# A gated mix of linear attention and experts on one Trainium2 core: pads put above the tiles, first-half queries first, loads moved

## The chip, the cores and the metric

The kernel runs on one core of a Trainium2 chip. The metric is the device time of one execution in microseconds, median over the runs; a lower time is better. The core's engines are TensorE (PE, with its weight loads shown as PEld), VectorE (DVE), ScalarE (ACT), GpSimd (POOL) and SyncE (SP). SP issues most DMAs, POOL the accumulating ones and some others. Each engine works through its own queue in order and waits on semaphores.

## The reference

Cut to what matters:

```python
S, D, F, E, H = 2048, 512, 1792, 8, 32          # one batch
phi = lambda t: where(t > 0, t + 1, exp(t)) + 1e-6

q, k, v = heads(x @ wqkv)                        # 32 heads of 16
kv, z   = einsum("sd,se->de", phi(k), v), phi(k).sum(0)
a = (phi(q) @ kv / (phi(q) @ z + 1e-6)) @ wo     # linear attention

w = softmax(x @ w_gate)                          # top 8 of 8: all experts
b = sum(w[:, e] * (silu(x @ w1[e]) @ w2[e]) for e in range(E))

g = sigmoid((x * gate_w).sum(-1))
out = g * a + (1 - g) * b
```

All in float32. The kernel keeps float32 accuracy by splitting each operand of a matmul into a high and a low part (type float32r) and adding three products, high by high, high by low and low by high.

## The kernel before, in words

**Products.** Each 256 x 256-blocked product is done by a scheme with seven products of half-size blocks in place of eight (Strassen's). So an expert's first layer ("up", x @ w1) works on seven combinations of x blocks and seven of weight blocks, and so does the second ("down", h @ w2). `mm3` (L57 to L60) is one such 128 x 128 by 128 x 512 product in its three split parts; lines L58, L59 and L60 are nearly all the matmuls of the kernel.

**Stages.** `keys` (L256) works over 16 row tiles: key projection, phi, and the sums y = phi(k)^T x. `experts` (L504) is then one long loop over steps `u` (L923).

**Halves, parts and groups.** The rows are two halves of 1024. A part is one expert (or the queries, `e == E`, which are treated as one more expert) for one half, `m.parts` (L102). An expert's part has 7 groups (pairs of 128 columns of F), a query part 2. `m.groups` (L109) lists them in the order of the loop: the first half's experts (56 groups), both query parts (2 groups each), the second half's experts (56). `m.G1` is the first group of the second half's queries, 58; from there on the x blocks of the second half (`n0` to `n6`) stand in place of the first half's (`x00`, `t1`, `x01`, `t3`, `x11`, `t5`, `t6`). `x_next` (L620) loads one of them from its stash in DRAM into the tiles that its predecessor leaves free; L987 to L996 say at which steps.

**Steps.** A group takes 7 steps, one up product each (6 matmuls), in `up` (L565). The down products run behind it: at step `u` the down tick is `clock(u)`, which is `u - LAG` in the first half and `u - LAG1` in the second, with LAG = 44 and LAG1 = 72. So steps 0 to 43 hold up products alone, then up and down run together, at the switch from first to second half there are 28 steps with up products alone, and at the end 72 with down products alone: 884 steps in all. `tick` (L747) does two down products (6 matmuls) with weights `w` and moving tiles `ho`; `evict` takes the results out of PSUM, scales them with the gate weights `wb` and adds them in DRAM (`acct`, on POOL's queue).

**What else a step does.** `load(g + 2)` and `prep(g + 1, k)` (L144, L175) load and split the weights of the coming groups: `rm` and `rs` are raw tiles, `o` and `oh` the split up weights, `ws` (or a spare `ho` tile, named `wx`, while `u < LAG - 8`) the split down weights, which go to a stash in DRAM (`w2stash`). `both` says that a group loads and stashes the down weights too; that is so in the first half only, and the second half reads the same stash. The queries' down weights are `wpd`, which `state` and `fold` make at steps 5 to 10. `load_w2` (L682) brings stashed weights back, three tiles of pool `w2p` in turn; from tile 377 on, every second one goes to ring "o" of pool `w1p`. `hidden` (L547) is Silu for an expert, one ACT instruction; for a query group it is `phi` (L71), two on ACT and one on DVE, and a store to `pqd`. ACT also copies PSUM banks and makes high parts (`high`), DVE low parts (`low_h`, L674) and adds (L612, L618).

**Queries and the end.** From step 461 on `queries_first` and `queries_last` turn the stored phi(q) into the attention's scaled inputs, four blocks of 512 rows, and put them back into `pqd`. In the last 28 ticks these are the moving tiles of the query parts' down products: `load_query` brings them (POOL's queue), `load_sums` the sums of the experts from `acct`, `rows` transposes the results and writes them out. `END` is tick 784.

**Memory.** Pools `const`, `xpool`, `w1p` and `hq` are stacked from the bottom of the memory. Pools `misc` (until step 17) and `w2p` (from then on) lie at its top. `pad` (L121) takes a tile of 24 float32, 96 bytes in each partition, and fills it with zeros on POOL; it is taken first in both of these pools. The tiles of such a pool lie in the order in which they are first taken, the first lowest, and the last ends at the top. In the built program the three tiles of `w2p` start at bytes 217056, 221152 and 225248 of each partition, that is 480 past a multiple of 512; the x tiles, `o`, `ho`, `ws`, raw and `r` tiles start 128 past one; tiles of `keys`' own pool that hold row tiles 12 to 15 and phi(k) start at a multiple of 512.

## Time and profile before

| | us |
|---|---|
| median of 3 runs | 2406.38 |
| lowest, highest | 2404.95, 2407.12 |
| profiled execution, its own time | 2408.38 |
| its span, first to last instruction | 2406.5 |
| `keys`, to the first up product | 100 |
| steps with up products alone, to the first down product | 100 to 182 |
| a group of 7 steps with up and down products | 19.37 |
| a group of up products alone | 9.52 |
| last down product | 2398 |

The granted clock of PE was 0.997 over the span. How to read the profile's rows: a group row gives line, engine, operation, out<-in by tile names, shapes and count, then busy time and mean length in ns of one, then the idle time of the engine before them and what ended it. A matmul's length is from its start to its modelled end and overlaps with the next one's; so rates are read from starts. A window row gives a stretch, its length, then busy us and number of instructions of PE, PEld, DVE, ACT and POOL, the granted clock, the busy share of the 16 DMA engines and the GB/s they moved. A timeline row gives start, length and the instruction, with the idle time before it in brackets. A wait row gives who waited for whom: us in total, times, the longest. A row of DMA issues gives the issuing queue, count, size and the median us from issue to landing.

### The profile page before, as it was taken

The page shows a single profiled execution, that of the slowest core. Times are in us where ns is not written, and L with a number is a line of the kernel's source. Part 1 is how long each engine was busy: PE and PEld are TensorE (multiplying, and loading weights), DVE is VectorE, ACT ScalarE, POOL GpSimd, SP SyncE. Part 2 cuts the span into 40 slices and gives each one's busy share as a digit, 9 for nine tenths or more (in the row PEclk, how much of TensorE's full clock was granted, in tenths as well). Part 3 has the DMA queues.
Part 4 walks back from the last instruction along what each step waited for, and adds up shares of the span by engine and source line. Part 5 has one row for each costly group of instructions (what it writes and reads, how often), then busy time and mean ns, then how long its engine had stood idle before and what let it go on. Part 6 is the DMA issues. An engine that isn't in the chain of part 4 may idle for free. (4 is left out here: it accounts for less than half of the span.)

```text
span 2406.5 us, 31379 instructions
## 1 busy us (share of the span) xinstructions
PE 2378.6 (99%) x10483; PEld 1936.1 (80%) x10483; DVE 1829.2 (76%) x3107; ACT 1414.8 (59%) x2650; POOL 151.8 (6%) x218
## 2 busy tenths in 40 slices
PE   8999999999999999999999999999999999999998
PEld 8878888888888888888788888888888888888876
DVE  6788888888888888888776767677676666766678
ACT  6676666666666666666656555555555555555454
POOL 1110000000000000000110000000000000000021
PEclk9999999999999999999999999999999999999999
DMA  7898888979888888879864444554545454454577
GB/s 219 263 300 253 266 266 261 274 249 279 255 262 263 263 273 257 273 254 273 288 208 121 143 139 167 146 162 149 167 153 142 137 144 142 142 148 132 140 272 269
DMA packets 296529, 512.31 MB, mean 213 GB/s; under 512 B 24224, under 2 KB 192048, under 8 KB 295984
## 3 DMA queue, kind: packets, MB, share of 16 engines
q1 hardware_dynamic: 273536, 463.84, 58.5%
q0 software_dynamic: 22832, 46.49, 10.0%
q8 instruction: 82, 1.34, 0.2%
q14 instruction: 79, 0.65, 0.1%
HBM read 344.61 MB, written 161.42 MB: 210 GB/s over the span
## 5 line engine op out<-in xcount | busy, mean ns | idle before, releaser
L58 PE MATMUL p<-ho,w 128*128 128x512 f32 x1624 | 645.7, 398 | 2.5 <-ACT p L63 1.6
L60 PE MATMUL p<-ho,w 128*128 128x512 f32 x1624 | 645.3, 397 | 0.0
L59 PE MATMUL p<-ho,w 128*128 128x512 f32 x1624 | 638.9, 393 | 0.0
L674 DVE TENSOR_TENSOR ho<-s,ho 128x512 fp32r<-128x512 f32 x784 | 536.2, 685 | 56.4 <-ACT ho L63 54.8
L63 ACT ACTIVATE ho<-s 128x512 fp32r<-128x512 f32 x784 | 486.5, 621 | 18.8 <-PE p L60 11.7
L58 PEld LDWEIGHTS p<-ho,w 128*128 128x128 f32 x1624 | 305.1, 188 | 76.3 <-ACT p L63 6.2
L60 PEld LDWEIGHTS p<-ho,w 128*128 128x128 f32 x1624 | 304.9, 188 | 74.3
L59 PEld LDWEIGHTS p<-ho,w 128*128 128x128 f32 x1624 | 305.5, 188 | 71.5
L550 ACT ACTIVATE s<-s 128x512 f32<-128x512 f32 x224 | 141.6, 632 | 282.8 <-DVE s L612 201.7
L612 DVE TENSOR_TENSOR s<-c,s 128x512 f32<-128x512 f32 x116 | 80.2, 691 | 151.5 <-PE c L60 147.2
L63 ACT ACTIVATE o<-rm 128x512 fp32r<-128x512 f32 x240 | 136.6, 570 | 86.0 <-PE a L60 65.4
L63 ACT ACTIVATE o<-rs 128x512 fp32r<-128x512 f32 x224 | 127.4, 569 | 67.4 <-PE a L60 63.8
L63 ACT ACTIVATE ws<-rm 128x512 fp32r<-128x512 f32 (+1 forms) x217 | 122.4, 571 | 63.4 <-DMA w2stash<-ws 56.4
L618 DVE TENSOR_TENSOR s<-a,s 128x512 f32<-128x512 f32 x116 | 80.1, 691 | 81.5 <-PE a L60 81.4
L550 ACT ACTIVATE s<-b 128x512 f32<-128x512 f32 x112 | 67.2, 600 | 114.5 <-PE b L60 102.2
L63 ACT ACTIVATE s<-a 128x512 f32<-128x512 f32 x116 | 69.3, 597 | 98.8 <-PE a L60 98.8
L190 DVE TENSOR_TENSOR o<-rs,o 128x512 fp32r<-128x512 f32 x168 | 114.8, 683 | 13.8 <-ACT o L63 13.0
L190 DVE TENSOR_TENSOR o<-rm,o 128x512 fp32r<-128x512 f32 x180 | 123.1, 684 | 1.3 <-ACT o L63 1.2
L208 DVE TENSOR_TENSOR ws<-rm,ws 128x512 fp32r<-128x512 f32 x164 | 112.3, 685 | 7.7 <-ACT ws L63 7.7
L63 ACT ACTIVATE s<-c 128x512 f32<-128x512 f32 x116 | 69.1, 595 | 27.0 <-PE c L60 26.9
L63 ACT ACTIVATE b<-a 128x512 f32<-128x512 f32 x116 | 67.1, 579 | 23.9 <-PE a L60 23.8
L708 POOL DMA_DIRECT2D acct<-c x28 | 24.0, 856 | 864.2 <-DVE c L704 639.2
(291 smaller groups left out, 4525.2 us busy)
## 6 DMA issues: line engine op xcount, KB each, us to landing
w<-w2stash SPq DMA_DIRECT2D x406, 512.0 KB, 3.9
w2stash<-ws SPq DMA_DIRECT2D x381, 256.0 KB, 4.4
rm<-wm SPq DMA_DIRECT2D x224, 256.0 KB, 5.4
rs<-wm SPq DMA_DIRECT2D x112, 256.0 KB, 3.7
wb<-wgtd SPq DMA_DIRECT2D x16, 512.0 KB, 5.0
acct<-c POOLq DMA_DIRECT2D x28, 256.0 KB, 5.6
acct<-d POOLq DMA_DIRECT2D x28, 256.0 KB, 5.4
acct<-k POOLq DMA_DIRECT2D x28, 256.0 KB, 5.4
```

The lines of the kernel that those rows point to most:

```text
L58: nc.tensor.matmul(ps, wh, xh, start=start, stop=False, skip_group_check=True)
L59: nc.tensor.matmul(ps, wh, xl, start=False, stop=False, skip_group_check=True)
L60: nc.tensor.matmul(ps, wlo, xh, start=False, stop=stop, skip_group_check=True)
L63: nc.scalar.activation(dst, src, AF.Copy, scale=scale, bias=bias)
L190: v.tensor_sub(two(o, 1), src, f32(two(o, 0)))
L208: v.tensor_sub(two(w, 1), src, f32(two(w, 0)))
L550: nc.scalar.activation(dst, src, AF.Silu)
L612: v.tensor_add(sn[g, 2], bank[g, "c"], sn[g, 2])
L618: v.tensor_add(sn[g, 3], bank[g, "a"], sn[g, 3])
L674: v.tensor_sub(h[:, 1], s, f32(h[:, 0]))
L708: nc.gpsimd.dma_start(m.acct[part.h, j, dt], s, accum_op=ALU.add)
```

## The change

1. `pad` is taken last in each of the two pools instead of first: in `misc` behind `sp`, which is itself now taken before the pad, and in `w2p` when all three `w2` tiles have been taken. In the built program the `w2` tiles then start at bytes 216960, 221056 and 225152, 384 past a multiple of 512; tiles of `misc` lie 96 bytes lower too.
2. The first half's queries come first in the order of groups; the second half's stay at the switch. LAG becomes 58 (LAG1 stays 72), so the stretch of up products alone is 58 steps at the start and 14 at the switch. Since `wpd` is not there yet at the start, the queries' down weights are loaded and stashed with the second half's query groups (`with_second`); the smaller raw tiles `rs` begin two groups later.
3. At the switch each x block is loaded at the step in which its predecessor is last used, steps 0, 2, 3, 4, 5, 6 of the group before and step 1 of group G1.
4. At the end the loads of queries and of the first half's sums begin at ticks 744 and 748 instead of 762 and 772, one every two ticks.

```diff
-    for i in (*range(E), 2 * E, 2 * E + 1, *range(E, 2 * E)):
+    for i in (2 * E, *range(E), 2 * E + 1, *range(E, 2 * E)):
...
     m.pad = pad
-    pad(m.misc)
...
+    def with_second(part):
+        return (part.e == E) == (part.h == 1)
...
         part, q = m.groups[g]
-        both = part.h == 0
-        if part.e < E and not both:
+        both = with_second(part)
+        if g >= m.G1 + 4:
             r = w1p.tile([P, 2 * D], F32, name=f"rs{g}", tag="ws", bufs=2)
...
         r = raw[g]
-        both = part.h == 0
+        both = with_second(part)
...
+    sp = sf_tile("sp")[:NH, :].rearrange("p (c f) -> p c f", c=KT)
+    m.pad(misc)
...
-    sp = sf_tile("sp")[:NH, :].rearrange("p (c f) -> p c f", c=KT)
...
-    LAG = 44
-    LAG1 = LAG + 28
+    LAG = 44 + 14
+    LAG1 = LAG + 14
...
             m.w2p = ctx.enter_context(tc.tile_pool(name="w2p", bufs=1, side="right", reuse_waits="tile"))
-            m.pad(m.w2p)
...
             load_w2(loaded)
             loaded += 1
-        if g == G1 - 1:
-            if k in (0, 3, 5):
-                x_next((0, 1, 2)[(0, 3, 5).index(k)])
-            if k == 6:
-                x_next(3)
-        if g == G1:
-            if k == 0:
-                x_next(4)
-            if k == 1:
-                x_next(5), x_next(6)
+            if loaded == 3:
+                m.pad(m.w2p)
+        if g == G1 - 1 and k != 1:
+            x_next(max(k - 1, 0))
+        if g == G1 and k == 1:
+            x_next(6)
...
-        if -22 <= at < -14:
-            load_query(0, at + 22)
-        if -8 <= at < 0:
-            load_query(1, at + 8)
-        if at in (-12, -10):
-            load_sums(0, (at + 12) // 2)
+        if at in (-40, -32):
+            load_sums(0, (at + 40) // 8)
+        if -36 <= at < -20 and at % 2 == 0:
+            load_query(0, (at + 36) // 2)
+        if -18 <= at < -2 and at % 2 == 0:
+            load_query(1, (at + 18) // 2)
```

## The prediction

> **What bounds the kernel now.** I read the page first, then windows of the loop, then single matmul starts, then the waits of the three places where TensorE (PE) pauses.

> ```profile
> span 2406.5 us, 31379 instructions
> PE 2378.6 (99%) x10483; PEld 1936.1 (80%) x10483; DVE 1829.2 (76%) x3107; ACT 1414.8 (59%) x2650; POOL 151.8 (6%) x218
> L58 PE MATMUL p<-ho,w 128*128 128x512 f32 x1624 | 645.7, 398 | 2.5 <-ACT p L63 1.6
> ```

> PE is busy 99% of the span and its largest group waits 2.5 us in all, so time can only come from the rate of the matmuls and from a few pauses. The windows give the rate; x counts matmuls, and behind PEld the weight loads, one for each matmul.

> ```profile
> 300.00:1000.00 700.00, 700.00 (x3038) 569.98 (x3037) 583.77 (x966) 444.13 (x838) 34.13 (x40) 1.00 0.86 264
> 1283.50:1309.50 26.00, 26.00 (x116) 21.54 (x115) 16.87 (x32) 16.26 (x30) 0.00 (x0) 1.00 0.40 129
> ```

> With up and down products mixed a matmul takes 700/3037 = 230.5 ns; in a stretch of up products alone 26.00/115 = 226.1 ns. The clock is 1.00 in both. Single starts show where the difference sits:

> ```profile
> 250.31 0.39 PE L58 MATMUL a<-t5h,o 128*128 128x512 f32 x1
> 251.68 0.39 PE L58 MATMUL p<-ho,w 128*128 128x512 f32 x1
> 253.07 0.39 PE L58 MATMUL a<-x00h,o 128*128 128x512 f32 x1
> ...
> 2346.08 0.39 PE L58 MATMUL p<-ho,w 128*128 128x512 f32 x1
> 2348.89 0.40 PE L58 MATMUL p<-ho,w 128*128 128x512 f32 x1
> 2351.62 0.39 PE L58 MATMUL p<-ho,w 128*128 128x512 f32 x1
> 2354.43 0.40 PE L58 MATMUL p<-ho,w 128*128 128x512 f32 x1
> ```

> Six up products take 1.37 us, six down products 1.39. Near the end only down products run, in sets of twelve that change place: there every second `w2` tile comes from ring "o" of pool `w1p` (load_w2, `i > ENDS and i % 2`), the others from `w2p`. Twelve with `w2p` weights take 2.81 us (from 2346.08), twelve with ring-"o" weights 2.73 (from 2348.89), then 2.81 again. Same shape, line and moving tiles: only the place of the weights differs. In the built program `ho`, `o` and the loop's x tiles all start 128 bytes past a multiple of 512 in their partition, the `w2p` tiles 480 past. I call weights' start minus moving tile's start, modulo 512, the distance: 0 for up products and ring "o", 352 for `w2p`.

> **The pads.** `pad` is 96 bytes. The pools on the right hold their first tile lowest and end at the top of the memory, so a pad taken first moves nothing; taken last it lowers all others by 96: `w2` from 480 past to 384 past, distance 256. No loop matmul of before has 256; the nearest rows:

> ```profile
> 43.60 0.40 PE L58 MATMUL y<-pkh,xt 128*128 128x512 f32 x1
> 46.39 0.28 PE L382 MATMUL g<-g,x10h 128*128 128x256 f32 x1
> 97.53 0.39 PE L58 MATMUL y<-pkh,xt 128*128 128x512 f32 x1
> 100.26 0.39 PE L562 MATMUL b<-x00h,o 128*128 128x512 f32 x1
> 1454.08 0.62 PE L878 MATMUL dn<-az 128*64 128x512 f32 x2
> 1454.54 0.40 PE L58 MATMUL b<-n2h,o 128*128 128x512 f32 x1
> 1457.32 0.62 PE L878 MATMUL dn<-az 128*64 128x512 f32 x2
> 1457.77 0.40 PE L58 MATMUL a<-n3h,o 128*128 128x512 f32 x1
> ```

> The twelve y matmuls at 43.60 have distance 128 (xt at 128, pkh at 0) and take 2.79 us; those at 97.53 have distance 0 and take 2.73. So a multiple of 128 alone isn't enough. The dn pairs decide: the weights of step s start s*256 bytes into `az`, so distance is 0 at 1454.08 (s=0) and 256 at 1457.32 (s=1), and the pairs take 0.46 and 0.45 us. I take 256 to act like 0, with less than full trust, as dn loads 64 columns and not 128. From both sides: a gain down to the 226.1 of the up products, or none; a loss stands under the rivals. I take 226.7 (2.72/12), between 226.1 and the 227.5 of the set at 2348.89, which begins behind a slow one. Up and down run together in 740 of the loop's 884 steps (812 up less 72 up alone, same count after), 12 matmuls each: 8880 x (230.5 - 226.7) = 34 us. Down products alone with `w2p` weights: 36 of the last 72 steps at 0.04 us (half of 2.81 - 2.73) = 1.4; the last ones are paced by VectorE (DVE), so 1. Sum -35.

> [...]

> **Queries first, and the stall at 168 us.** Groups 0 and 1 become first-half queries, down products begin at step 58 instead of 44, and the gap of up-only steps at the switch shrinks from 28 to 14; the work on PE is the same. What it touches:

> ```profile
> 100.00:182.50 82.50, 73.24 (x317) 57.74 (x316) 64.05 (x114) 58.36 (x112) 10.27 (x22) 0.96 0.93 297
> 140.00:150.00 10.00, 10.00 (x46) 8.18 (x45) 9.57 (x16) 8.11 (x17) 6.74 (x15) 1.00 0.96 296
> 170.00:180.00 10.00, 7.53 (x20) 5.64 (x21) 8.75 (x14) 8.37 (x16) 0.00 (x0) 0.66 0.81 256
> ...
> ACT ws L63 <- DMA w2stash<-ws: 10.1, 4, 4.8
> DVE gat L811 <- ACT gat L810: 3.7, 1, 3.7
> PE c L58 <- ACT s L63: 3.1, 1, 3.1
> PE b L58 <- ACT b L63: 2.2, 1, 2.2
> PE a L58 <- DVE s L618: 1.6, 1, 1.6
> PE a L58 <- ACT s L63: 0.7, 1, 0.7
> PE kv L780 <- DMA wv<-wv: 1.6, 2, 0.8
> ...
> wb<-wgtd SPq DMA_DIRECT2D x16, 512.0 KB, 5.0
> ...
> 1163.68 0.69 DVE L74 SCALAR_TENSOR_TENSOR e<-e,s 128x512 f32<-128x512 f32 x1 [1.36 <-ACT s L73]
> ```

> Removed: 2.2 us at step 0, where ScalarE (ACT) was held by the stash of group 0's w2 half, which a query group hasn't; 1.6 for `wv`, which stood behind four such stashes on SP's queue; and most of the pause at 168: ACT waited 4.8 us for a stash when the spare `ws` tiles ended, PE 3.1 and 0.7, and between 170 and 180 the clock was 0.66: 20 matmuls where 43 fit, (43 - 20) x 0.23 = 5.3 us lost, of which 10 - 7.53 = 2.5 idle, so 2.8 by the rate. After, the spare tiles end 14 steps (19 us) later against `wb`'s broadcast (5.0 us to land) and the gates' rows, which held the queue up, so it has had time to drain; of 3.1 + 0.7 + 2.8 = 6.6 I keep 1.1. Removed in all 2.2 + 1.6 + 5.5 = 9.3. The raw tiles of a query group are half as many bytes, so the loads at the start only get lighter.

> Added: a query group needs phi instead of one Silu: for each of 4 tiles one more ACT operation and one on DVE (0.60 back to back), and for two of them DVE stands 1.36 us while ACT makes both halves (last row). That is 4 x 0.60 + 2 x 1.36 = 5.1 a group, 10.2 for both. Formerly this lay beside down products, in steps of 2.77 us; now it lies in steps of 1.36, where DVE is already busy 9.57 of 10 us. Queued behind each such wait are the adds of L618 (now L624), which free PE's bank a within one step. The 8 stores to `pqd` move with them on POOL's queue, ahead of the gates' rows and so of `wb`, which is first read some 40 steps later. Cover: DVE's 3.7 us for the gates' exponentials, since two table loads fall away. 10.2 - 3.7 = 6.5 added. Net -2.8; bounds -9.3 (all added work covered) and +8 (nothing removed but the 2.2, all 10.2 exposed).

> **Loads at the switch.**

> ```profile
> 1166.80:1186.70 19.90, 19.75 (x84) 15.80 (x85) 15.37 (x27) 14.18 (x27) 2.16 (x4) 1.00 0.83 298
> 1186.70:1213.10 26.40, 22.85 (x85) 17.25 (x84) 16.83 (x30) 14.68 (x28) 4.49 (x7) 0.87 1.03 381
> 1213.10:1232.50 19.40, 19.40 (x86) 15.77 (x85) 13.19 (x25) 12.79 (x24) 1.62 (x3) 1.00 0.47 172
> ...
> PE c L58 <- DMA n4h<-xstash: 3.0, 1, 3.0
> ...
> n4h<-xstash SPq DMA_DIRECT2D x1, 512.0 KB, 13.4
> w<-w2stash SPq DMA_DIRECT2D x2, 512.0 KB, 12.7
> ```

> A group of 7 steps takes 19.4 us, the two at the switch 0.5 and 7.0 more: x part 4 was asked for 5 steps (14 us) ahead, landed 13.4 us after its issue, and the pause halved the clock again (0.87). After, each part is asked for right behind its predecessor's last use, 7 steps (19 us) ahead. But the group before the switch now moves 12 x loads (6 MB), 3.5 w loads (1.8), raw tiles (1) and the stash of a query group with its `wpd` half (1.8): 10.6 MB, some 28 us at 381 GB/s in 19 us. The backlog of 9 us and 3 us of landing stay under 19, so x is in time; `w` loads queue behind them on SP, with about 4 steps (11 us) of lead against 12.7 seen. I leave 2 us of the 7.5: -5.5; bounds -7.5 and +2 (the old pause back and the `w` wait on top). Groups 60 and 61 keep the larger raw tile; they load the same bytes, no cost.

> **Loads at the end.**

> ```profile
> DVE tl L724 <- PE p L60: 2.8, 3, 1.1
> ...
> 2361.90 8.66 DMA tl<-acct
> ```

> The chain ends through these loads, yet the adds that use them waited for PE; the loads came just in time behind a busy DVE. 24 loads move earlier on POOL's queue (16 of queries, 8 of sums), past accumulating stores; the tiles whose slots they take were last read before, so POOL isn't held. If that cover were gone, DVE would wait for one load, about 1 us. 0, bounds -1.5 and +0.5.

> **Sum.** -35 - 2.8 - 5.5 = -43 on the profiled execution's 2408.4 us (span 2406.5 and 1.9 around it), which lies 2.0 above the median of 2406.4: 2365 - 2 = 2363.

> **Rivals.** (1) The pads change nothing in time: distance 256 disturbs like 128 and 352. For it: the y set at 128. Against: the dn pairs. Then only -8.3 is left: 2398. [...] (2) Slower: at distance 256 weights and moving data meet worse than at 352, in all 740 steps. Down products now take 233 ns (1.39 to 1.40 us for six); at 238, about the slowest single step in the y set and the w2p sets, 4440 of them cost +22, less 8: 2420. It decides the sign from 236 on, where 4440 x 3 ns outweigh the 8 and the noise. For it: nothing shows 256 with 128 columns; against: the same dn pairs. (3) The start gets worse: phi's waits make pauses of over 3 us in groups 1 and 2, and the clock halves as at 170 to 180. That is +8 instead of -2.8: 2374.

> [...]

> **How the numbers follow.** Forecast 0.66 (own range 2352 to 2374, the start's and the switch's bounds and 226.1 not all at once), rival 3 0.11, rival 1 0.16, rival 2 0.07. The measurement tells about 0.2% (4.8 us). Faster: 0.66 + 0.11 + 0.13 of rival 1 = 0.90; same 0.03; slower 0.07. The range 2352 to 2397 holds the forecast, rival 3 and half of rival 1, some 0.82.

> **What would show it.** Right: six down products in 1.36 us, a group every 19.04, about 3088 weight loads between 300 and 1000; no wait for n4h; no clock under 0.9 at the switch. At the start, waits of PE on L624's adds in groups 1 and 2 and none on `wv`. Wrong: 230.5 ns a matmul as before (rival 1), over 232 (rival 2), or a clock of 0.66 near 130 us (rival 3).

## The result, and the profile after

| | before | after |
|---|---|---|
| median, us | 2406.75 (4 runs, 2404.95 to 2408.24) | 2379.61 (4 runs, 2378.16 to 2380.45) |
| profiled execution, us | 2408.38 | 2379.32 |
| ratio after to before | | 0.9887, 95% interval 0.987 to 0.9904 |

The change takes 27 us off, where 43 had been forecast. The page of after, its span, PE's busy time and its largest group:

```profile
span 2377.6 us, 31361 instructions
...
PE 2344.5 (99%) x10483; PEld 1936.6 (81%) x10483; DVE 1828.4 (77%) x3107; ACT 1409.6 (59%) x2648; POOL 152.8 (6%) x218
...
L58 PE MATMUL p<-ho,w 128*128 128x512 f32 x1624 | 635.6, 391 | 8.8 <-DMA w<-w2stash 5.8
```

The down products' matmuls became shorter (391 ns for 398), but they now wait 8.8 us where it was 2.5, and 5.8 of it for loads of `w`, which before showed none. Windows of after (stretch, length, busy us and instructions of PE, PEld, DVE, ACT, POOL, clock, DMA share, GB/s): the loop, a piece of the start, and the three groups around the switch.

```profile
300.00:1000.00 700.00, 700.00 (x3090) 579.63 (x3089) 593.26 (x983) 449.97 (x850) 33.98 (x40) 1.00 0.87 268
1126.80:1145.84 19.04, 19.04 (x85) 15.77 (x84) 13.33 (x22) 8.27 (x16) 1.69 (x2) 1.00 1.04 326
1145.84:1179.27 33.43, 23.43 (x86) 17.92 (x84) 17.64 (x29) 14.96 (x28) 1.14 (x2) 0.80 0.86 327
1179.27:1198.69 19.42, 19.35 (x85) 15.68 (x85) 15.37 (x27) 13.72 (x27) 2.17 (x4) 1.00 0.72 228
127.60:137.60 10.00, 6.79 (x19) 4.96 (x18) 6.59 (x14) 7.58 (x16) 1.29 (x3) 0.66 0.58 185
```

The loop runs at 700/3089 = 226.6 ns a matmul (before 230.5) and a group takes 19.04 us (before 19.37). The bad group of the switch takes 33.43 us, where the worst one took 26.40: 14.4 more than a group of the loop, 10.0 of it idle (33.43 - 23.43) and 4.4 at a clock of 0.80. Single starts of PE, a set of six down products first, then the pauses (in brackets the idle time and what ended it):

```profile
252.32 0.39 PE L58 MATMUL p<-ho,w 128*128 128x512 f32 x1
...
253.68 0.39 PE L58 MATMUL c<-t1h,o 128*128 128x512 f32 x1
...
131.20 0.79 PE L58 MATMUL a<-t6h,o 128*128 128x512 f32 x1 [3.21 <-DVE s L624]
...
1159.44 0.79 PE L58 MATMUL p<-ho,w 128*128 128x512 f32 x1 [3.89 <-DMA w<-w2stash]
1166.17 0.80 PE L58 MATMUL c<-n4h,o 128*128 128x512 f32 x1 [3.80 <-ACT s L63]
1179.27 0.50 PE L58 MATMUL a<-n6h,o 128*128 128x512 f32 x1 [2.31 <-DVE s L624]
...
2266.68 0.47 PE L58 MATMUL p<-ho,w 128*128 128x512 f32 x1 [0.41 <-DMA w<-w2stash]
2270.49 0.47 PE L58 MATMUL p<-ho,w 128*128 128x512 f32 x1 [1.48 <-DMA w<-w2stash]
```

Six down products take 1.36 us (252.32 to 253.68; before 1.39). At the switch there is no wait for `n4h` as data any more; the pause ahead of its first matmul is one for ACT. What held ACT shows in the waits of after between 1150 and 1182 us (total, times, longest):

```profile
ACT ws L63 <- DMA w2stash<-ws: 13.4, 2, 8.6
```

ACT stood 13.4 us at the tiles `ws`, which come free only when the stash of the queries' down weights has landed. From 1149.70 to 1163.48 us it ran a single operation of 0.42 us; its queue behind that, with the copy of bank c that PE needs (at 1165.53), waited along. At the end, where before shows no wait of PE on loads, two short ones are new.

To compare kernels by stage I add up, over all gaps of more than 0.30 us between starts of PE's matmuls, what exceeds 0.23 us; this holds pauses and the half clock (in after 0.50 from 131.20 to 135.00, for one) alike. Each cell is one profiled execution, in us; the ranges of the start are those of all kernels with that order:

| kernel | start (100 to 300) | switch (1100 to 1320) | end (from 2200) |
|---|---|---|---|
| before | 16.0 | 9.1 | 6.2 |
| after | 12.3 | 16.5 | 9.0 |
| old order, five kernels | 12.6 to 16.0, mean 14.8 | | |
| new order with phi and the gates at step 11, five kernels | 12.2 to 12.6, mean 12.4 | | |

### The profile page after: what moved, and what is told of

It reads as the page before. It is cut to its first block, busy times and chain, and to the rows that moved or that the text cites. A ratio compares the mean times of both kernels' runs of the same rounds, so it can differ in the third digit from the quotient of the medians.

```text
span 2377.6 us, 31361 instructions
## 1 busy us (share of the span) xinstructions
PE 2344.5 (99%) x10483; PEld 1936.6 (81%) x10483; DVE 1828.4 (77%) x3107; ACT 1409.6 (59%) x2648; POOL 152.8 (6%) x218
## 3 DMA queue, kind: packets, MB, share of 16 engines
q0 software_dynamic: 22832, 46.49, 10.1%
## 5 line engine op out<-in xcount | busy, mean ns | idle before, releaser
L58 PE MATMUL p<-ho,w 128*128 128x512 f32 x1624 | 635.6, 391 | 8.8 <-DMA w<-w2stash 5.8
L59 PE MATMUL p<-ho,w 128*128 128x512 f32 x1624 | 632.9, 390 | 0.0
L60 PE MATMUL p<-ho,w 128*128 128x512 f32 x1624 | 632.8, 390 | 0.0
L63 ACT ACTIVATE ho<-s 128x512 fp32r<-128x512 f32 x784 | 486.6, 621 | 18.2 <-PE p L60 12.6
L58 PEld LDWEIGHTS p<-ho,w 128*128 128x128 f32 x1624 | 305.3, 188 | 78.3 <-ACT p L63 6.8
L60 PEld LDWEIGHTS p<-ho,w 128*128 128x128 f32 x1624 | 305.4, 188 | 63.7
L63 ACT ACTIVATE o<-rm 128x512 fp32r<-128x512 f32 x248 | 141.1, 569 | 83.2 <-PE a L60 59.1
L618 DVE TENSOR_TENSOR s<-c,s 128x512 f32<-128x512 f32 x116 | 80.0, 690 | 136.5 <-PE c L60 132.3
L63 ACT ACTIVATE ws<-rm 128x512 fp32r<-128x512 f32 x214 | 120.7, 571 | 83.5 <-DMA w2stash<-ws 72.9
L63 ACT ACTIVATE o<-rs 128x512 fp32r<-128x512 f32 x216 | 122.7, 568 | 65.4 <-PE a L60 62.7
L624 DVE TENSOR_TENSOR s<-a,s 128x512 f32<-128x512 f32 x116 | 80.0, 690 | 70.5 <-PE a L60 70.2
L63 ACT ACTIVATE s<-a 128x512 f32<-128x512 f32 x116 | 69.1, 596 | 90.7 <-PE a L60 90.6
L63 ACT ACTIVATE s<-c 128x512 f32<-128x512 f32 x116 | 69.0, 595 | 26.0 <-PE c L60 26.0
L63 ACT ACTIVATE b<-a 128x512 f32<-128x512 f32 x116 | 67.1, 578 | 21.1 <-PE a L60 20.7
## 6 DMA issues: line engine op xcount, KB each, us to landing
w<-w2stash SPq DMA_DIRECT2D x406, 512.0 KB, 3.9
wb<-wgtd SPq DMA_DIRECT2D x16, 512.0 KB, 5.1
```

Source lines behind the costliest of these rows:

```text
L58: nc.tensor.matmul(ps, wh, xh, start=start, stop=False, skip_group_check=True)
L59: nc.tensor.matmul(ps, wh, xl, start=False, stop=False, skip_group_check=True)
L60: nc.tensor.matmul(ps, wlo, xh, start=False, stop=stop, skip_group_check=True)
L63: nc.scalar.activation(dst, src, AF.Copy, scale=scale, bias=bias)
L618: v.tensor_add(sn[g, 2], bank[g, "c"], sn[g, 2])
L624: v.tensor_add(sn[g, 3], bank[g, "a"], sn[g, 3])
```

## Experiments

**The pads alone.** Before, with `pad` taken last in both pools:

```diff
     m.pad = pad
-    pad(m.misc)
...
+    sp = sf_tile("sp")[:NH, :].rearrange("p (c f) -> p c f", c=KT)
+    m.pad(misc)
...
-            m.pad(m.w2p)
...
             loaded += 1
+            if loaded == 3:
+                m.pad(m.w2p)
```

> Before with the pads taken last and nothing else. If the pads are worth what the sum said (34 us in the mixed steps, 1 behind them) and the other three edits lose about 8 us together, this kernel takes 2406.75 - 35 = 2372, a group of mixed steps 19.04 us, and the pauses at 100 (2.2), 168 (3.1 and a clock near 0.66) and at the switch (7.5 us over two groups) are those of before. If the pads are worth only the 27 us by which the whole change is faster, because the faster loop runs into its loads more often, it takes about 2380, with new waits of PE on DMA in the loop.

2371.7 us (2368.89 to 2373.1), ratio 0.9853 [0.9838, 0.9868], 35.6 below before. The loop's window and the waits of PE around the switch, of this kernel:

```profile
300.00:1000.00 700.00, 700.00 (x3089) 579.60 (x3089) 591.18 (x980) 450.07 (x851) 34.11 (x40) 1.00 0.88 269
```

```profile
PE c L58 <- DMA n4h<-xstash: 2.4, 1, 2.4
PE c L59 <- DMA n4l<-xstash: 1.4, 1, 1.4
```

So the pads are worth what the sum gave them, the old pauses stay, and the other three edits together lose 8 us (2379.6 - 2371.7).

**The old x loads.** After, with the steps of before for `x_next`:

```diff
-        if g == G1 - 1 and k != 1:
-            x_next(max(k - 1, 0))
-        if g == G1 and k == 1:
-            x_next(6)
+        if g == G1 - 1:
+            if k in (0, 3, 5):
+                x_next((0, 1, 2)[(0, 3, 5).index(k)])
+            if k == 6:
+                x_next(3)
+        if g == G1:
+            if k == 0:
+                x_next(4)
+            if k == 1:
+                x_next(5), x_next(6)
```

> After, with the x blocks of the second half loaded at the steps of before (0, 3, 5, 6 of the group before the switch, 0 and 1, 1 of the next). Theory A, the sooner x loads fill the queue and make the w loads late: the wait of 3.9 us on w at the switch goes, the two groups there lose 5 to 8 us instead of 15, time 2370 to 2373. Theory B, the queries' stash that now lies at the switch fills it: the two groups still lose 12 us or more, PE still waits on ACT that waits for its stash, time 2377 to 2383.

**The old order.** After, with order, `LAG` and the stash of before:

```diff
-    for i in (2 * E, *range(E), 2 * E + 1, *range(E, 2 * E)):
+    for i in (*range(E), 2 * E, 2 * E + 1, *range(E, 2 * E)):
...
-        return (part.e == E) == (part.h == 1)
+        return part.h == 0
...
-    LAG = 44 + 14
-    LAG1 = LAG + 14
+    LAG = 44
+    LAG1 = LAG + 28
```

> After, with the order of the groups of before: both query parts at the switch, the stash with the first half's, LAG 44. Pads, x loads and the loads at the end as after. Theory A (sooner x loads are to blame): a wait on w of 3 us or more stays at the switch, 10 to 15 us are lost there, and the time is 2378 to 2384, as the start has its old pauses back. Theory B (the stash in groups 57 and 58 is to blame): the switch loses 0 to 4 us, the start has its old pauses (about the same sum as the new ones), time 2366 to 2371.

Old x 2375.37 us (2374.54 to 2376.43), switch 12.1; old order 2374.31 us (2371.78 to 2375.36), switch 10.2. Neither of the two theories holds alone. From 9.1 before, the stash alone adds some 3 us, the sooner x loads alone some 1, both together 7.4: they fall into the same 40 us, and each costs little there without the other. (The four kernels with the old order and the old x loads lose 7.6 to 10.2 there, so the 1 of the x loads is no more than their spread; the 3 of the stash is.) PE's waits at the switch, with the stash alone (old x):

```profile
PE p L58 <- DMA w<-w2stash: 1.5, 1, 1.5
PE a L58 <- DVE s L624: 1.5, 1, 1.5
PE c L58 <- ACT s L63: 1.4, 1, 1.4
PE a L58 <- DMA n3h<-xstash: 1.3, 1, 1.3
```

and with the sooner x loads alone (old order):

```profile
PE p L58 <- DMA w<-w2stash: 5.1, 2, 4.2
PE a L58 <- DVE s L624: 0.9, 1, 0.9
```

Here x is in time, as forecast, and the 5.1 us on `w` are the price of it: the old wait of 2.4 and 1.4 on `n4` has changed its name. With the old order the start lost 12.6 us here against 15.0 with the pads alone, though nothing of the start differs between them; so a stage's loss can move by 2 us from run to run, and only means over several kernels say what queries first is worth: 12.4 - 14.8 = -2.4.

**The old loads at the end.** After, with `load_query` and `load_sums` at the ticks of before:

```diff
-        if at in (-40, -32):
-            load_sums(0, (at + 40) // 8)
-        if -36 <= at < -20 and at % 2 == 0:
-            load_query(0, (at + 36) // 2)
-        if -18 <= at < -2 and at % 2 == 0:
-            load_query(1, (at + 18) // 2)
+        if -22 <= at < -14:
+            load_query(0, at + 22)
+        if -8 <= at < 0:
+            load_query(1, at + 8)
+        if at in (-12, -10):
+            load_sums(0, (at + 12) // 2)
```

> After, with the loads of queries and sums at the ticks of before. If the spread loads delay the w loads at 2266 to 2269 us (0.4 and 1.5 us of waits there), these waits go and the time is 2377 to 2378. If those waits come from something else they stay, and the time is 2379 to 2380.5.

2376.95 us (2376.38 to 2377.84), and the waits on `w` there are gone. The DMA issues between 2244 and 2270 us (queue, count, size, median us to landing), first of after, then of this kernel:

```profile
w<-w2stash SPq DMA_DIRECT2D x6, 512.0 KB, 5.4
tl<-acct POOLq DMA_DIRECT2D x8, 256.0 KB, 5.5
q<-pqd POOLq DMA_DIRECT2D x3, 256.0 KB, 6.0
```

```profile
w<-w2stash SPq DMA_DIRECT2D x7, 512.0 KB, 3.2
```

The spread loads meet the `w` loads just where down products begin to run alone and a `w` load has half the time, and they lengthen it from 3.2 to 5.4 us. Nor are they spread in time: POOL stands 12.0 us ahead of a load of `q` (for what, the profile does not show) and then issues what has piled up, six loads within 2.7 us from 2259.8 on. Over all kernels with the old loads the end loses 6.2 to 6.7 us, with the new ones 8.6 to 10.6.

**The stash later.** After, with the stash of the queries' down weights carried by the second half's groups G1+2 and G1+3 (experts that stash nothing themselves); groups up to G1+5 keep the larger raw tile:

```diff
-    def with_second(part):
-        return (part.e == E) == (part.h == 1)
+    def second(g):
+        part, q = m.groups[g]
+        if m.G1 + 2 <= g < m.G1 + 4:
+            return m.parts[2 * E + 1], g - m.G1 - 2
+        return (part, q) if part.e < E and part.h == 0 else None
...
-        if g >= m.G1 + 4:
+        if g >= m.G1 + 6:
...
         def stash(prod, src):
+            part, q = both
```

> After, with the stash of the queries' down weights carried by groups 60 and 61 instead of 58 and 59, two groups behind the x loads. If the pile-up at the switch is the sum of both loads (10.2 us lost with the sooner x loads alone, 12.1 with the stash alone, 16.5 with both), PE's wait on ACT that waits for a stash goes, the switch loses 6 to 10 us, and the time is 2370 to 2374. If the stash stalls ACT wherever it lies in the second half, new waits come in groups 59 and 60 and the time stays within 2377 to 2381.

2369.55 us (2368.84 to 2371.25), ratio 0.9843 [0.9828, 0.9858]; the switch loses 6.6 us, 9.9 less than after and 2.5 less than before. Waits of PE there:

```profile
PE a L58 <- DVE s L628: 1.7, 1, 1.7
PE p L58 <- ACT p L63: 1.3, 1, 1.3
PE p L58 <- DMA w<-w2stash: 1.2, 2, 0.9
```

No pause there is followed by a lower clock (1.00 in all windows from 1126 to 1212), and the stash two groups later stalls nobody. So it was the meeting of the two loads, not the stash as such.

**The x loads on POOL's queue.** The kernel just above, with the old loads at the end and

```diff
-            nc.sync.dma_start(f32(XO[1][i][c]).rearrange("p k t -> p (k t)"), m.xstash[i, c])
+            nc.gpsimd.dma_start(f32(XO[1][i][c]).rearrange("p k t -> p (k t)"), m.xstash[i, c])
```

> After, with the stash as in the run before, the x loads on POOL's queue in place of SP's, and the loads at the end as before. If the w loads are late because they stand behind 512 KB x loads in one queue, they now land in 4 to 6 us, no wait of PE on w is left at the switch, it loses 0 to 4 us, and with 2.4 us back at the end the time is 2363 to 2367. If the DMA engines' rate sets it and not the queue's order, w or x still come late, the switch loses 6 to 10 us, and the time is 2368 to 2372. If POOL, which waits at each x load until PE has read the old block, holds up the accumulating stores, waits of ACT or DVE on tiles c, d, e appear in groups 57 and 58.

2372.19 us (2371.77 to 2373.2): worse, by 5 us with the end's gain counted. Issues between 1140 and 1165 us of this kernel, and its wait:

```profile
w<-w2stash SPq DMA_DIRECT2D x4, 512.0 KB, 9.8
n4h<-xstash POOLq DMA_DIRECT2D x1, 512.0 KB, 14.8
```

```profile
PE p L58 <- DMA w<-w2stash: 3.8, 1, 3.8
```

With all on SP's queue the same `w` loads had taken 8.6 us and `n4h` 10.2. Without the x loads in their queue the `w` loads landed no sooner (9.8 us), and the DMA engines moved 405 GB/s in these 25 us with all on SP's queue and 406 with the x loads on POOL's. The second theory, that the rate sets it and not the queue's order, fits, though the switch loses 10.5 us and the time is 2372.2, both just above what it allowed. Waits of the accumulating stores grew by nothing.

**The gates behind the add.** After, with the gates' 2.7 us on DVE moved behind step 13:

```diff
-        if u == 11:
-            gates()
-        if u == 13:
-            normaliser()
-        if u == 15:
-            gate_rows()
+        if u == 11:
+            normaliser()
+        if u == 13:
+            gates()
+        if u == 16:
+            gate_rows()
```

> After, with the gates' work on DVE (2.7 us in a row, at step 11, ahead of the add that the product at 131.2 waits for) moved behind step 13, the normaliser's (0.9 us) moved to 11, the gates' rows to 16. If the pause of 3.2 us at 127.6 comes from the gates standing ahead of that add, it shrinks to 1 us or less, the half clock behind it (2.6 us) goes, and the time is 2374 to 2376. If phi's own waits make it, it stays and the time is 2378.5 to 2380.5.

2378.66 us (2376.57 to 2380.72), no difference that can be told. PE's waits from 100 to 200 us:

```profile
PE a L58 <- ACT s L63: 3.0, 2, 2.3
PE a L58 <- DVE s L624: 2.2, 2, 1.4
```

The pause on L624's add shrank from 3.2 to 1.4, and the half clock behind it went; but a pause of 2.3 us for ACT came up at 139.9, and now the half clock (0.50) follows that one, for 3.4 us. The gates did stand ahead of that add, but the start still loses 11.6 us, where kernels with the gates at step 11 lose 12.4: most of what it is short of is something else.

**Phi left out.** After, with one Silu in place of phi in the first half's query groups; it leaves out phi there, so it computes something else:

```diff
-        if dst is src:
-            dst = r_tile(f"e{g}_{f}{t}")
-        phi(dst, src)
+        if part.h == 0:
+            nc.scalar.activation(dst, src, AF.Silu)
+        else:
+            if dst is src:
+                dst = r_tile(f"e{g}_{f}{t}")
+            phi(dst, src)
```

> After, with Silu in one instruction in place of phi for the first half's query groups; it leaves out phi there, the stores to pqd stay. If phi's waits cost what the sum had (6.5 us added), the pause at 127.6 and its half clock go, the losses from 100 to 200 us fall from 12.3 to about 6, and the time is 2373 to 2375. If the start is bound by DVE and by the stash whatever the groups are, other pauses take their place, the losses stay at 10 us or more and the time is 2377 to 2380.

2376.69 us in one run; the start loses 9.3 us, between the two theories. So phi's share of it is about 12.4 - 9.3 = 3.1 us, as far as one execution tells.

**Three distances in one kernel.** The pads alone, each of the three `w2` tiles with its own pad behind it, 32, 32 and 24 floats. They then lie at distances 0, 128 and 256:

```diff
             loaded += 1
-            if loaded == 3:
-                m.pad(m.w2p)
+            if loaded <= 3:
+                nc.gpsimd.memset(m.w2p.tile([P, (32, 32, 24)[loaded - 1]], F32, name=f"pad{loaded}", tag=f"pad{loaded}", bufs=1), 0.0)
```

> The kernel with the pads alone, but with pads of 128, 128 and 96 bytes behind the three w2 tiles, so that these lie at distances 0, 128 and 256 from the moving tiles. If the rate goes by the distance modulo 256, down products with the tiles at 0 and 256 take 1.36 us for six and those at 128 about 1.39, as the y set at 128 did; time 2371.7 plus a third of some 30 us, so 2380 to 2384. If 128 is as good as 256 for weights of 128 columns and the y set was slow for another reason, all three take 1.36 and the time is 2371 to 2373.

2387.45 us in one run. Starts of PE: a set at 128, one at 256, one at 0, each with the up product behind it:

```profile
600.80 0.40 PE L58 MATMUL p<-ho,w 128*128 128x512 f32 x1
...
602.20 0.39 PE L58 MATMUL c<-t1h,o 128*128 128x512 f32 x1
...
603.56 0.39 PE L58 MATMUL p<-ho,w 128*128 128x512 f32 x1
...
604.92 0.39 PE L58 MATMUL b<-x01h,o 128*128 128x512 f32 x1
...
609.00 0.39 PE L58 MATMUL p<-ho,w 128*128 128x512 f32 x1
...
610.36 0.39 PE L58 MATMUL c<-x11h,o 128*128 128x512 f32 x1
```

1.40, 1.36 and 1.36 us. In one and the same kernel, by the mean over some 1550 matmuls each: 0 gives 227.1 ns, 256 gives 227.3, 128 gives 233.8 (352, in before: 233.5). So the first theory holds for the rate. The time is 3.5 us above the 2384 that it allowed, and no run here says why. The same with pads of 40, 32 and 8 floats, that is 32, 192 and 320:

> The pads alone, the three w2 tiles at distances 32, 192 and 320 from the moving tiles. If only multiples of 256 are free, all three take 232 to 236 ns a matmul, a group 19.3 to 19.4 us, and the time is 2400 to 2408. If small distances or some other multiples of 64 are free too, one or two of the three take 227, and the time is 2380 to 2395.

2406.3 us in one run, as much as before. Starts at 32, then at 192:

```profile
601.35 0.39 PE L58 MATMUL p<-ho,w 128*128 128x512 f32 x1
...
602.75 0.39 PE L58 MATMUL a<-x00h,o 128*128 128x512 f32 x1
...
604.11 0.39 PE L58 MATMUL p<-ho,w 128*128 128x512 f32 x1
...
605.49 0.39 PE L58 MATMUL a<-t6h,o 128*128 128x512 f32 x1
...
613.76 0.39 PE L58 MATMUL a<-t3h,o 128*128 128x512 f32 x1
...
615.16 0.39 PE L58 MATMUL p<-ho,w 128*128 128x512 f32 x1
```

1.40 us for the six at 32 (mean 232.4 ns), 1.38 at 192 (229.0); those at 320 mean 233.0. So 192 lies in between, which neither theory had. The last two rows show six up products in 1.40, though their own distance is 0 as ever and those from 602.75 take 1.36: here the disturbance reaches into the matmuls between the down products. How, no run here settles.

**All that helped together.** The stash later, the old loads at the end and the gates behind step 13:

> After, with the stash in groups 60 and 61 (2369.6 alone), the loads at the end as before (-2.4 to -2.7 alone) and the gates' work behind step 13 (-0.7 us of pauses alone). If the three stages are independent, the time is 2369.6 - 2.5 - 0.7 = 2366.4, within 2365 to 2368, below both the kernel after (2379.6) and the pads alone (2371.7). If what is gained at one place is waited for at the next, it stays at 2369 to 2372.

2367.12 us (5 runs, 2365.12 to 2367.92), ratio 0.9841 [0.9828, 0.9855]: 12.5 below after, 4.6 below the pads alone. These kernels ran beside different runs of before: against its own, this one gains 38.8 us (2405.91 - 2367.12) and the pads alone 35.6, 3.2 apart, and the intervals of the two ratios overlap. The profiled execution is the fastest of the five. In it the same pause of 2.3 us (at 139.3) leaves the clock at 1.00, and the start loses 10.1. In its page the largest wait of the down products is one for ACT; 1.3 us for `w` are left at the switch.

```profile
span 2363.3 us, 31376 instructions
...
L58 PE MATMUL p<-ho,w 128*128 128x512 f32 x1624 | 634.6, 391 | 4.8 <-ACT p L63 2.7
```

## Why the prediction was right in part

| term | forecast, us | measured | from |
|---|---|---|---|
| pads | -35 | -35.6 | the pads alone |
| queries first, start | -2.8 | -2.4 | means of five starts each |
| loads at the switch | -5.5 | +7.4 | after less before, 16.5 - 9.1 |
| loads at the end | 0 | +2.6 | mean of six kernels with the new loads, 9.1, less seven with the old, 6.5 |
| sum | -43 | -28 | -27.1 by medians, -29.1 by profiled executions |

**The pads: right in step and size.** Six down products take 1.36 us, a group 19.04, and 3089 weight loads fall between 300 and 1000 us, each as written. That the dn pairs could speak for weights of 128 columns was the weakest link; the kernel with three distances shows it held. Rivals 1 and 2 fall with it: 256 is neither like 128 nor worse than 352.

The pads alone, which move tiles by 96 bytes and change no work, took off 35.6 us, so here the place of the weights counts. Why the distance matters, no run here shows.

**The start: right in sum, with two terms too large.** Phi was to add 6.5 us and adds 3.1; what the new order takes away was to be 9.3, and is 14.8 - 9.3 = 5.5, with 9.3 the loss of the start without phi. The errors cancel. The waits on `wv` and at step 0 are gone as written, and L624's add is waited for in group 1 (131.20). But the stall on the stash at 168 moved on to 187 to 195 us, rather than leaving 1.1. Rival 3's sign was there too, a clock of 0.66 from 127.6 to 137.6, and still the start came out no worse: the pause (3.21 us) and the half clock behind it (0.50) came about, their price did not. In the kernel with the x loads on POOL's queue the same pause of 3.2 us left the clock at 1.00, and the start lost 12.2 all the same.

**The switch: the step that failed.** "The backlog of 9 us and 3 us of landing stay under 19, so x is in time; `w` loads queue behind them on SP, with about 4 steps (11 us) of lead against 12.7 seen. I leave 2 us of the 7.5: -5.5". The first half held. The price did not, by 13 us, and for two reasons. The wait on `w` was 3.9 us. And the sum counted the queries' stash as bytes in the queue only, not as a thing for which ACT waits before it can take the next `ws` tile: 13.4 us, in which all of ACT's later work stood, and with it PE for 3.8. The third pause, 2.3 us for DVE's add, is mostly not the stash's: with the stash moved away 1.7 are left. Half the clock (0.50 from 1159.4 to 1170.0) behind the first two pauses cost 4.4 us more, and the sign "no clock under 0.9 at the switch" failed with 0.80. The bound of +2 was too narrow for the same reason: it took the pauses one by one, while stash and x loads are each cheap alone (+3 and +1) and dear together. Moving the stash away gave 9.9 us back.

**The end: a cover that was not one.** It had "the loads came just in time behind a busy DVE" and bounds of -1.5 and +0.5 for DVE's own waits. What the moved loads meet is another queue's: the `w` loads, which landed in 5.4 us beside them and in 3.2 without, though the DMA engines were only 0.47 busy from 2230 to 2270 us with the old loads. The step that looked at POOL's queue alone and not at who shares the engines mis-sized the term by 2.6 us.

So the direction rests on the pads alone, 36 us; the other three edits gave back some 8 of it. The 2379.6 us lie outside the 2352 to 2374 that the forecast gave to its own mechanism. They lie inside the range up to 2397, which was drawn that wide to take in half of rival 1, and rival 1 did not come about; that the range held them is in part luck.

## What to carry to other kernels

Where matmuls of one shape run at different rates, compare the addresses of their weights and moving data first: taking a 96-byte pad last instead of first was worth 1.5% here, and costs nothing. A load that is moved must be priced against everything that moves in its new place (the moved loads at the end took the `w` loads there from 3.2 to 5.4 us), and a store whose tile an engine waits for again is a wait on that engine, not only bytes (13.4 us of ACT at the switch). Two moves that each cost little can cost much where they meet (+3 and +1 us alone, +7.4 together), so try them one at a time and together.

## What the runs showed of the hardware

The length of a pause alone doesn't tell whether PE's clock halves behind it. These windows begin behind pauses of 3.1 us (the pads alone), 3.2 (x loads on POOL's queue), 2.3 (gates behind the add) and 2.0 (three distances):

```profile
106.36:112.00 5.64, 5.11 (x24) 4.04 (x25) 5.50 (x10) 4.99 (x9) 0.00 (x0) 1.00 1.00 286
131.92:138.00 6.08, 6.08 (x28) 4.96 (x29) 4.80 (x11) 6.03 (x13) 1.08 (x2) 1.00 0.87 284
139.75:143.16 3.41, 3.27 (x8) 2.63 (x9) 2.50 (x5) 2.27 (x5) 1.73 (x4) 0.50 1.05 357
106.24:109.65 3.41, 3.41 (x9) 2.64 (x8) 3.31 (x7) 3.38 (x6) 0.00 (x0) 0.50 0.85 258
```

The two longer ones left the clock at 1.00, the two shorter ones were followed by 0.50. In after, 3.2 us (at 131.2) were followed by 0.50 until 135.0 (0.66 over the ten us from 127.6), and 2.3 us (at 1179.3) by 1.00. In before, 3.1 us (at 171.8) had 0.66 behind them, as the prediction says, with 0.50 from 174 to 180. What else decides, no run here shows.

Loads on POOL's queue did not leave SP's loads more of the DMA engines: 512 KB on SP took 9.8 us beside them, 8.6 with all of them on SP.
